# Two gates of an adaLN block: column sums on VectorE, spread over the partitions through DRAM

## The chip, the cores and the metric

The kernel runs on one core of a Trainium2 chip. The metric is the device time of one execution in microseconds (us). Engines are named as the profile names them: PE (TensorE), PEld (its weight loads), DVE (VectorE), ACT (ScalarE), POOL (GpSimd), SP (SyncE, which issues every DMA of this kernel). L12 is line 12 of the kernel before.

## What is computed

One block over x of shape (1, 2048, 512), with six rows of 512 made from a condition vector c of 512 elements:

```python
mod = (_silu(c) @ w_mod).reshape(c.shape[0], 6, 1, -1)
sa, ca, ga, sb, cb, gb = (mod[:, 0], mod[:, 1], mod[:, 2], mod[:, 3], mod[:, 4], mod[:, 5])
h = _layernorm(x, axis=-1) * (1 + ca) + sa
x = x + ga * _A_ref(h, A_w_r, A_w_i)      # rfft2, times w_r + i w_i, irfft2
h = _layernorm(x, axis=-1) * (1 + cb) + sb
x = x + gb * _B_ref(h, B_w1, B_b1, B_w2)  # 512 -> 1376, Mish, 1376 -> 512
return x
```

The two gates are ga and gb. Both multiply along the 512 features, which lie along the free axis of x in SBUF, so that each of the 128 partitions needs the whole row of 512.

## The kernel before

The work is three phases, each with a schedule written out by hand: an engine's instructions stand in the order of the program, and an instruction waits for semaphores of the others.

**First phase.** Forward transform over the features and over the long axis, one step for each of 16 slices of x. It also makes ca and sa.

**Second phase** (L534 to L596). The 64 complex columns are taken in 17 groups, in the order `seq`. In step s of its loop (L575) DVE multiplies group s with the spectral weights (`p2_prod`, L498), PE makes the products of group s+1 (`p2_mul`, L482), transposes group s+3 in (`p2_in`, L461), transposes group s-2 back (`p2_back`, L515) and makes the last products of group s-3 (`p2_out`, L528). POOL and, for a few groups, DVE combine the products to y (L503, L504). ACT copies the banks out (L464, L518) and stores d (L381, L382). A PSUM tag ("A" to "D") has two banks, so `p2_mul` of group s+1 waits until `p2_prod` of group s-1 has read its bank.

The rows 2 to 5 of `mod` are made beside it, in 16 pieces of w_mod of 128 x 512 (four for each row, 256 KB each). `mod_fetch(s + 2)` issues the loads into four buffers (L541), so a load waits for the sum four pieces earlier. `mod_late(s)` takes a piece on DVE, after `p2_prod` in program order; `when` (L534) gives the step of each piece: ga's four in steps 3, 4, 5 and 6, those of sb and cb in steps 6, 7, 8, 9, 9, 10, 11 and 12, and gb's four in steps 12, 13, 14 and 16. There are two forms:

- `mod_column` (L110), for sb and cb: a piece holds 128 of the features on its partitions and the 512 elements of the contraction along the free axis; one DVE instruction multiplies by silu(c), which lies on every partition (`scb`), and sums along the free axis into a column of `cols`.
- `mod_step` (L98 for the first piece, L100 for the others), for ga and gb: a piece holds 128 elements of the contraction on its partitions and the 512 features along the free axis; DVE multiplies it by silu(c) for each partition and adds it to a 128 x 512 accumulator, `modr[:, 0]` for ga and `modr[:, 2]` for gb.

The sum over the partitions that is left is a PE product with a 128 x 128 matrix of ones, which also puts the row on every partition: `mod_gate` (L553) in step 7 for ga, into a bank of tag "A", behind it `kiv`, the last transform's matrix, times the bank on DVE (L554); and `apply_gate` (L558) after the last step for gb, into a bank of tag "B", with a copy to `gbr` by ACT (L559). In step 9 SP issues the two loads of `kc` (1 MB each, L595), behind the eleventh piece of w_mod.

**Third phase** (L902 to L930). In 16 steps the inverse transform over the long axis with `kc` (`p3_col`, L663 and L664) and over the features with `kiv` (`p3_row`, L673), with x += (L676) and the second norm's sums. SP loads w1 in 12 pieces of up to 256 KB into two buffers (`load_w1`, L615; each is let go by `split_w1` of two pieces earlier, which ACT and POOL do in L621 and L622) and w2 (L703). Then follows the feed-forward part, in 8 blocks of 6 steps; `gbr` is first read there.

SP issues DMAs in program order; a DMA waits in the queue for what it needs, and those behind it wait too.

Of the kernel before, what the change touches and what calls it, by code (L numbers as in the profile page):

```python
# [31 lines left out]
def tile_spectral_block(ctx: ExitStack, tc: tile.TileContext, x_d, w1_d, b1_d, w2_d,  # L32
                        c_d, xt_d, wm_d, wq_d, wz_d, kr_d, km_d, kc_d, ki_d, kf_d, kv_d, kw_d, kp_d, out_d):
    nc = tc.nc
# [3 lines left out]
    base = ctx.enter_context(tc.tile_pool(name="base", bufs=1))  # L38
    small = ctx.enter_context(tc.tile_pool(name="small", bufs=4))
    work = ctx.enter_context(tc.tile_pool(name="work", bufs=2))  # L40
    big = ctx.enter_context(tc.tile_pool(name="big", bufs=1))

    psum = ctx.enter_context(tc.tile_pool(name="psum", bufs=2, space=bass.MemoryType.PSUM))

    def pipeline(count, *steps):
# [5 lines left out]
    def bank(tag):  # L51
        return psum.tile([P, 512], F32, name="bank", tag=tag)
# [8 lines left out]
    sc = base.tile([P, 4], F32, name="sc")  # L61
    ident = base.tile([P, P], F32, name="ident")
    kiv = base.tile([P, 4, P], F32, name="kiv")
    ones = base.tile([P, P], F32, name="ones")
    b1n = base.tile([P, NF], F32, name="b1n")
    modr = base.tile([P, 3, D], F32, name="modr")
    gbr = modr[:, 2]
    krs = modr[:, 0].rearrange("p (j e) -> p j e", j=4)
    scb = modr[:, 1]
    cols = base.tile([P, 2, 2, 4], F32, name="cols")  # L70
# [2 lines left out]
    nmr = base.tile([P, N2], F32, name="nmr")  # L73
    eps = base.tile([P, 1], F32, name="eps")

    saz = base.tile([P, NQ], F32, name="saz")
    mraw = big.tile([P, N2, 256], F32, name="mraw", tag="da")
    mring = big.tile([P, 8, 2, 384], F32R, name="mring", tag="db")
# [12 lines left out]
    kw = pw.tile([96, P], F32, name="kw")  # L91
    kb = modr[:, 2]
    hring = first.enter_context(tc.tile_pool(name="hring", bufs=1))

    def mod_step(acc, w, k, eng):
        one = sc[:, k:k + 1]
        if k == 0:
            eng.tensor_scalar(acc, w, one, 0.0, op0=ALU.mult, op1=ALU.add)  # L98
        else:
            eng.scalar_tensor_tensor(acc, w, one, acc, op0=ALU.mult, op1=ALU.add)  # L100

    def scale_spread():
        ps = bank("D")
# [5 lines left out]
    def mod_column(w, out, by, waste):  # L109
        nc.vector.scalar_tensor_tensor(waste, w, by, scb, op0=ALU.mult, op1=ALU.mult, accum_out=out)  # L110

    def plus_one(dst, src):
        nc.scalar.activation(dst, src, AF.Identity, bias=ones[:, 0:1])
# [45 lines left out]
    st = {}  # L159
# [294 lines left out]
    def p2_in(g):  # L454
        if g == 0:
            return z_in()
        q0, nq = groups[g]
        w = nq * P
        ps = bank("A")
        for i in range(nq):  # L460
            nc.tensor.transpose(ps[:, i * P:(i + 1) * P],  # L461
                                a_sb[:, q0 + i, :, :].rearrange("p n e -> p (n e)"), ident)
        z = zbuf(g)
        nc.scalar.copy(z[:, 0:w], ps[:, 0:w])  # L464
        st["z", g] = z
        if seq.index(g) >= 2:
            p2_shift(g)

    def p2_shift(g):
        q0, nq = groups[g]  # L470
        zc = st["z", g][:, 0:nq * P:P]
        nc.gpsimd.tensor_tensor(zc, zc, saz[:, q0:q0 + nq], op=ALU.add)

    def p2_mul(g):
        if g == 0:
            return z_mul()
        q0, nq = groups[g]
        w = nq * P
        z = st.pop(("z", g))
        pb = bank("B")  # L480
        for i in range(nq):
            nc.tensor.matmul(pb[:, 0:w].rearrange("p (e q) -> p e q", q=nq)[:, :, i], z[:, i * P:(i + 1) * P],  # L482
                             kf[:, 0:128], start=True, stop=True)
        st["pb", g] = pb
# [22 lines left out]
    def p2_back(g):  # L507
        if g == 0:
            return z_back()
        q0, nq = groups[g]  # L510
        w = nq * P
        y = st.pop(("y", g))
        pc = bank("C")
        for i in range(nq):
            nc.tensor.transpose(pc[:, i * P:(i + 1) * P], y[:, 0:w].rearrange("p (e q) -> p e q", q=nq)[:, :, i],  # L515
                                ident)
        t = buf("t")
        nc.scalar.copy(t[:, 0:w], pc[:, 0:w])  # L518
        st["t", g] = t
# [18 lines left out]
    def mod_fetch(s):  # L538
        for which, k in work_mod.get(s, ()):
            w = late[which, k] = hring.tile([P, 512], F32, name="wm", tag="ht", bufs=4)  # L540
            nc.sync.dma_start(w, wm_d[2 + which, k])  # L541

    def mod_late(s):
        for which, k in work_mod[s]:
            w = late.pop((which, k))
            if which in (1, 2):
                mod_column(w, cols[:, 1, which - 1, k:k + 1], 1.0, w)
            else:
                mod_step(modr[:, 0 if which == 0 else 2], w, k, nc.vector)

    def mod_gate():
        ga = bank("A")
        nc.tensor.matmul(ga, ones, modr[:, 0], start=True, stop=True)  # L553
        nc.vector.tensor_tensor(kiv, kiv, ga.rearrange("p (b a) -> p b a", b=4), op=ALU.mult)  # L554

    def apply_gate():
        gb = bank("B")
        nc.tensor.matmul(gb, ones, modr[:, 2], start=True, stop=True)  # L558
        nc.scalar.copy(gbr, gb)  # L559

    kc = []
    wqb = pw.tile([P, 8, 2, 64, 4], F32, name="wqb", tag="half")
    with tc.manual_schedule():
        for i in range(8):
            nc.sync.dma_start(wqb[:, i], wq_d[8 + i])
        for i in range(LEAD):
            p2_in(seq[i])
            if i == 1:
                for g in seq[:2]:
                    p2_shift(g)  # L570
            if i in (2, 4):
                p2_mul(seq[i // 2 - 1])
            if i == 3:
                p2_prod(seq[0])
        for s in range(len(seq) + 3):  # L575
            mod_fetch(s + 2)
            if 0 < s < len(seq):
                p2_prod(seq[s])
            if 2 <= s + 1 < len(seq):
                p2_mul(seq[s + 1])  # L580
            if LEAD <= s + 3 < len(seq):
                p2_in(seq[s + 3])
            mod_late(s)
            if 2 <= s < len(seq) + 2:
                p2_back(seq[s - 2])
            if s >= 3:
                p2_out(seq[s - 3])
            if s == 7:
                mod_gate()
            if s == 14:  # L590
                plus_one(cols[:, 1, 1, :], cols[:, 1, 1, :])
            if s == 9:
                for i, t in enumerate(("cr", "ci")):
                    kc.append(big.tile([P, N2, P], F32, name=f"kc{i}", tag=t))
                    nc.sync.dma_start(kc[i], kc_d[:, i, :, :])  # L595
        apply_gate()  # L596
    first.close()

    pm = ctx.enter_context(tc.tile_pool(name="pm", bufs=1))
# [8 lines left out]
    def piece(i):  # L608
        k, c = divmod(i, 3)
        return k, 512 * c, min(512 * c + 512, F)  # L610

    def load_w1(i):
        k, lo, hi = piece(i)
        r = buf("g2")[:, 0:hi - lo]
        nc.sync.dma_start(r, w1v[:, k, lo:hi])  # L615
        st["w1", i] = r
# [285 lines left out]
    for s in range(N2 + 1):  # L902
        if s < N2:
            p3_col(s)
        if s < 12:
            load_w1(s)
        if s >= 1:
            p3_row(s - 1)
        if s in (3, 5):
            norm_scale(s - 3, s - 1)  # L910
        if s in (9, 13):
            norm_scale(s - 5, s - 1)
        if s == 15:
# [140 lines left out]
def _layout(x, w_r, w_i, w_mod):  # L1054
    import numpy as np

    w = np.stack([w_r, w_i])
    p, k, q = np.arange(128), np.arange(16), np.arange(64)
    own = p[:, None] + 128 * k
    far = (128 - p[:, None] + 128 * k) % 2048  # L1060

    def pick(row, col):
        return w[:, row[:, :, None], col]

    wq = np.stack([pick(own, q), pick(own, q + 128), pick(far, 256 - q), pick(far, 128 - q)], 2)
    wz = np.concatenate([pick(own, np.array([0, 128])), pick(far, np.array([192, 64, 256]))], 3)
    wq = wq.reshape(2, 128, 4, 16, 16, 4).transpose(4, 1, 0, 2, 3, 5).reshape(16, 128, 2, 64, 4)
    m = w_mod.reshape(128, 4, 6, 512).transpose(2, 1, 0, 3).copy()
    m[1:3] = m[1:3].reshape(2, 4, 128, 128, 4).swapaxes(3, 4).reshape(2, 4, 128, 512)
    t = w_mod.reshape(128, 4, 6, 512).transpose(2, 3, 1, 0).reshape(6, 512, 512)  # L1070
    m[0] = t[0].reshape(128, 4, 512).swapaxes(0, 1)
    m[3:5] = t[3:5].reshape(2, 4, 128, 512)
    xt = x.reshape(128, 16, 128, 4).transpose(1, 2, 3, 0)
    out = dict(x_t=xt, w_mod=m, w_q=wq, w_z=wz.transpose(1, 0, 3, 2))
    return {k: np.ascontiguousarray(v) for k, v in out.items()}
# [28 lines left out]
```

## Time and profile before

| what | us |
|---|---|
| median of 3 runs | 391.72 |
| lowest and highest of them | 391.29, 391.91 |
| the profiled execution's own time | 391.52 |
| its span, first to last instruction | 389.4 |
| PE busy | 383.1 |
| DVE busy | 298.8 |
| ACT busy | 247.9 |
| POOL busy | 96.1 |

The span is what the profile's rows add up to; 2.1 us of the profiled execution's time lie outside it. A row of the timeline has the start, the duration, the engine, the line and operation, the result and its inputs, and in brackets how long the engine had been idle and what released it. A row of the groups by line has the number of instructions and their least, median and greatest duration in ns. The rows of DMA issues have the size of each and the median time from issue to landing. The chain that ended last is followed back from the last instruction to what released each one.

### The profile page before, as it was taken

The page shows a single profiled execution, that of the slowest core. Times are in us where ns is not written, and L with a number is a line of the kernel's source. Part 1 is how long each engine was busy: PE and PEld are TensorE (multiplying, and loading weights), DVE is VectorE, ACT ScalarE, POOL GpSimd, SP SyncE. Part 2 cuts the span into 40 slices and gives each one's busy share as a digit, 9 for nine tenths or more (in the row PEclk, how much of TensorE's full clock was granted, in tenths as well). Part 3 has the DMA queues.
Part 4 walks back from the last instruction along what each step waited for, and adds up shares of the span by engine and source line. Part 5 has one row for each costly group of instructions (what it writes and reads, how often), then busy time and mean ns, then how long its engine had stood idle before and what let it go on. Part 6 is the DMA issues. An engine that isn't in the chain of part 4 may idle for free.

```text
span 389.4 us, 7386 instructions
## 1 busy us (share of the span) xinstructions
PE 383.1 (98%) x2752; PEld 355.4 (91%) x2752; DVE 298.8 (77%) x668; ACT 247.9 (64%) x546; POOL 96.1 (25%) x132
## 2 busy tenths in 40 slices
PE   8999999999999999999999999999999999999996
PEld 8889889999999998999998998999999999899984
DVE  2888978876299989887856965965966875987993
ACT  1798756678559648975855765674674674594751
POOL 0687737665077533300000000000000010017000
PEclk9999999999999999999999999999999999999999
DMA  7999993472132411100100100100100200123011
GB/s 237 383 323 339 347 344 109 133 300 63 47 124 78 145 49 28 56 3 0 56 0 3 54 2 0 56 0 2 55 2 0 76 0 2 46 65 106 3 54 54
DMA packets 21027, 36.44 MB, mean 94 GB/s; under 512 B 3680, under 2 KB 6592, under 8 KB 20736
## 3 DMA queue, kind: packets, MB, share of 16 engines
q1 hardware_dynamic: 20992, 35.98, 27.1%
q8 instruction: 21, 0.34, 0.3%
q14 instruction: 14, 0.11, 0.1%
HBM read 31.78 MB, written 4.19 MB: 92 GB/s over the span
## 4 chain that ended last, share of the span: by engine, by line
PE 86%; DMA 4%; DVE 3%; ACT 3%; issue 1%; SPq 1%; POOL 1%; POOLq 0%; DVEq 0%
PE bank L805 24%; PE bank L752 20%; PE bank L754 10%; PE bank L482 3%; PE bank L528 3%; PE bank L673 3%; PE bank L663 3%; PE bank L664 3%; PE bank L797 2%; PE bank L248 2%; DMA x<-in_A_x_dram 2%; PE bank L203 2%; PE bank L817 2%; PE bank L642 2%; PE bank L461 2%; DMA mraw<-in_km_dram 2%
## 5 line engine op out<-in xcount | busy, mean ns | idle before, releaser
L762 ACT ACTIVATE buf<-bank,b1n 128x256 f32<-128x256 f32 (+1 forms) x88 | 40.8, 472 | 66.8 <-PE bank L754 66.4
L763 DVE TENSOR_TENSOR buf<-buf,bank 128x256 f32<-128x256 f32 (+1 forms) x88 | 35.4, 417 | 38.6 <-ACT buf L762 38.6
L715 DVE TENSOR_TENSOR al<-buf,ah 128x512 fp32r<-128x512 f32 (+2 forms) x85 | 53.5, 653 | 0.7 <-ACT ah L714 0.7
L734 POOL TENSOR_TENSOR buf<-buf,modr 128x512 f32<-128x512 f32 (+1 forms) x3 | 3.9, 1292 | 183.0 <-DMA buf<-in_B_w_dram 175.7
L752 PE MATMUL bank<-h2e,w1h 128*128 128x512 f32 (+1 forms) x176 | 48.4, 397 | 0.0
L752 PE MATMUL bank<-h2o,w1h 128*128 128x512 f32 (+1 forms) x176 | 48.3, 396 | 0.0
L714 ACT CAST ah<-buf 128x512 fp32r<-128x512 f32 (+2 forms) x85 | 43.0, 548 | 1.2 <-DVE buf L779 1.2
L779 DVE TENSOR_TENSOR buf<-buf 128x128 f32<-128x128 f32 x148 | 39.9, 311 | 3.5 <-ACT buf L769 2.2
L769 ACT ACTIVATE buf<-buf 128x512 f32<-128x512 f32 (+1 forms) x48 | 28.6, 596 | 14.8 <-DVE buf L763 14.7
L805 PE MATMUL bank<-w2a,ah 128*128 128x256 f32 x161 | 34.9, 286 | 0.0
L752 PEld LDWEIGHTS bank<-h2o,w1h 128*128 128x128 f32 (+1 forms) x176 | 30.2, 187 | 4.5
L752 PEld LDWEIGHTS bank<-h2e,w1h 128*128 128x128 f32 (+1 forms) x176 | 30.1, 187 | 4.5
L805 PE MATMUL bank<-w2b,ah 128*128 128x256 f32 x147 | 31.8, 283 | 0.0
L754 PEld LDWEIGHTS bank<-h2o,w1l 128*128 128x128 f32 (+1 forms) x176 | 26.7, 185 | 4.2
L754 PEld LDWEIGHTS bank<-h2e,w1l 128*128 128x128 f32 (+1 forms) x176 | 26.7, 185 | 4.2
L754 PE MATMUL bank<-h2e,w1l 128*128 128x256 f32 (+1 forms) x176 | 27.8, 280 | 0.0
L754 PE MATMUL bank<-h2o,w1l 128*128 128x256 f32 (+1 forms) x176 | 27.8, 280 | 0.0
L805 PEld LDWEIGHTS bank<-w2a,ah 128*128 128x128 f32 x161 | 26.7, 191 | 0.0
L663 PE MATMUL bank<-kc,d 128*128 128x128 f32 x128 | 24.7, 275 | 0.0
L664 PE MATMUL bank<-kc,d 128*128 128x128 f32 x128 | 24.7, 275 | 0.0
L805 PEld LDWEIGHTS bank<-w2b,ah 128*128 128x128 f32 x147 | 24.6, 191 | 0.0
L117 DVE BATCH_NORM_STATS2 st<-x 128x6 f32<-128x512 f32 x32 | 22.1, 689 | 0.8 <-DMA x<-in_A_x_dram 0.4
(227 smaller groups left out, 1002.7 us busy)
## 6 DMA issues: line engine op xcount, KB each, us to landing
buf<-in_B_w_dram SPq DMA_DIRECT2D x20, 256.0 KB, 2.8
x<-in_A_x_dram SPq DMA_DIRECT2D x16, 256.0 KB, 4.9
xring<-in_x_t_dram SPq DMA_DIRECT2D x16, 256.0 KB, 5.1
wm<-in_w_mod_dram SPq DMA_DIRECT2D x16, 256.0 KB, 4.2
out_dram<-x SPq DMA_DIRECT2D x7, 512.0 KB, 2.6
mraw<-in_km_dram SPq DMA_DIRECT2D x16, 128.0 KB, 5.0
wqa<-in_w_q_dram SPq DMA_DIRECT2D x8, 256.0 KB, 4.8
wqb<-in_w_q_dram SPq DMA_DIRECT2D x8, 256.0 KB, 5.5
```

Source lines behind the costliest of these rows:

```text
L117: nc.vector.bn_stats(t, x[:, n, :])
L663: nc.tensor.matmul(o, dj[:, 0:128], kc[0][:, n, :], start=True, stop=False)
L664: nc.tensor.matmul(o, dj[:, 64:192], kc[1][:, n, :], start=False, stop=True)
L714: nc.scalar.copy(h, r)
L715: nc.vector.tensor_tensor(l, r, plain(h), op=ALU.subtract)
L752: nc.tensor.matmul(ps, w1h[:, k, fs], h[:, k], start=(k == 0), stop=False)
L754: nc.tensor.matmul(ps[:, 0:256], w1l[:, k, fs], h[:, k, 0], start=False, stop=(k == 3))
L762: nc.scalar.activation(o, ps[:, 256:], AF.Identity, bias=b1n[:rows, f:f + 1])
L763: nc.vector.tensor_tensor(o, o, ps[:, 0:256], op=ALU.add)
L769: nc.scalar.activation(o, o, AF.Mish)
L779: nc.vector.tensor_tensor(o, p, q, op=op)
L805: nc.tensor.matmul(o, a[p][:, e], w2[t][q][:, r], start=(own and half == 0 and t == 1 and i == 0), stop=(end and i == 2 and (n, half) != ( ...
```

## The change

ga and gb are summed as columns, by `mod_column`, like sb and cb: their pieces of w_mod are laid out by feature, and the sums go to a new tile `gcol` of 128 x 2 x 4 (feature 4p + k on partition p). Then two DMAs turn the column into a row on every partition: `flat` writes the 128 x 4 elements, 16 bytes from each partition, to a DRAM tile of 512 elements; `spread` reads these 2 KB once for each of the 128 partitions into `modr[:, 0]` (ga) or `gbr` (gb). Both are issued by SP; the second waits for the first to land. For ga they are issued in steps 8 and 9 of the second phase (behind the tenth piece of w_mod, and behind the eleventh, in front of `kc`), and kiv's multiply moves from step 7 to step 12, behind that step's two pieces. It reads `modr[:, 0]` in SBUF in place of a bank. For gb they are issued in steps 2 and 4 of the third phase, each behind that step's load of w1. Both products with ones and ACT's copy go.

```diff
+    dram = ctx.enter_context(tc.tile_pool(name="dram", bufs=1, space=bass.MemoryType.DRAM))
+    def flat(name, src, k=4):
+        t = dram.tile([1, P * k], F32, name=name)
+        nc.sync.dma_start(t.rearrange("b (p k) -> p (b k)", k=k), src)
+        return t
+    def spread(dst, t):
+        nc.sync.dma_start(dst, bass.AP(tensor=t.tensor, offset=t.offset, ap=[[0, P], [1, D]]))
...
+    gcol = base.tile([P, 2, 4], F32, name="gcol")
...
     def mod_late(s):
         for which, k in work_mod[s]:
             w = late.pop((which, k))
-            if which in (1, 2):
-                mod_column(w, cols[:, 1, which - 1, k:k + 1], 1.0, w)
-            else:
-                mod_step(modr[:, 0 if which == 0 else 2], w, k, nc.vector)
+            mod_column(w, cols[:, 1, which - 1, k:k + 1] if which in (1, 2) else gcol[:, which // 3, k:k + 1], 1.0, w)
     def mod_gate():
-        ga = bank("A")
-        nc.tensor.matmul(ga, ones, modr[:, 0], start=True, stop=True)
-        nc.vector.tensor_tensor(kiv, kiv, ga.rearrange("p (b a) -> p b a", b=4), op=ALU.mult)
-    def apply_gate():
-        gb = bank("B")
-        nc.tensor.matmul(gb, ones, modr[:, 2], start=True, stop=True)
-        nc.scalar.copy(gbr, gb)
+        ga = modr[:, 0]
+        nc.vector.tensor_tensor(kiv, kiv, ga.rearrange("p (a b) -> p b a", b=4), op=ALU.mult)
...
-            if s == 7:
+            if s == 8:
+                st["ga"] = flat("ga", gcol[:, 0])
+            if s == 9:
+                spread(modr[:, 0], st["ga"])
+            if s == 12:
                 mod_gate()
...
-        apply_gate()
...
         if s < 12:
             load_w1(s)
+        if s == 2:
+            st["gb"] = flat("gb", gcol[:, 1])
+        if s == 4:
+            spread(gbr, st["gb"])
```

On the host, w_mod's rows for ga and gb are stored by feature, like those of sb and cb, instead of by element of the contraction.

More of the change, by code (lines that the diff above doesn't have):

```diff
@@ L93, in tile_spectral_block @@
     hring = first.enter_context(tc.tile_pool(name="hring", bufs=1))
[L95 to L98, printed above, removed]
-        else:
-            eng.scalar_tensor_tensor(acc, w, one, acc, op0=ALU.mult, op1=ALU.add)
     def scale_spread():
@@ L545, in mod_late @@
             w = late.pop((which, k))
-            if which in (1, 2):
-                mod_column(w, cols[:, 1, which - 1, k:k + 1], 1.0, w)
-            else:
-                mod_step(modr[:, 0 if which == 0 else 2], w, k, nc.vector)
+            mod_column(w, cols[:, 1, which - 1, k:k + 1] if which in (1, 2) else gcol[:, which // 3, k:k + 1], 1.0, w)
     def mod_gate():
-        ga = bank("A")
-        nc.tensor.matmul(ga, ones, modr[:, 0], start=True, stop=True)
-        nc.vector.tensor_tensor(kiv, kiv, ga.rearrange("p (b a) -> p b a", b=4), op=ALU.mult)
-    def apply_gate():
-        gb = bank("B")
-        nc.tensor.matmul(gb, ones, modr[:, 2], start=True, stop=True)
-        nc.scalar.copy(gbr, gb)
+        ga = modr[:, 0]
+        nc.vector.tensor_tensor(kiv, kiv, ga.rearrange("p (a b) -> p b a", b=4), op=ALU.mult)
     kc = []
@@ L1068, in _layout @@
     m = w_mod.reshape(128, 4, 6, 512).transpose(2, 1, 0, 3).copy()
-    m[1:3] = m[1:3].reshape(2, 4, 128, 128, 4).swapaxes(3, 4).reshape(2, 4, 128, 512)
+    m[1] = m[1].reshape(4, 128, 128, 4).swapaxes(2, 3).reshape(4, 128, 512)
     t = w_mod.reshape(128, 4, 6, 512).transpose(2, 3, 1, 0).reshape(6, 512, 512)
-    m[0] = t[0].reshape(128, 4, 512).swapaxes(0, 1)
+    for i in (0, 2, 5):
+        m[i] = t[i].reshape(128, 4, 512).swapaxes(0, 1)
     m[3:5] = t[3:5].reshape(2, 4, 128, 512)
```

## Prediction

> **What bounds the kernel now.** I read the chain that ended last, then the stage in which the gates are made. PE (TensorE) carries 86% of the chain; a product taken off PE is worth its length, as long as PE isn't then held by something else.
>
> ```profile
> PE 86%; DMA 4%; DVE 3%; ACT 3%; issue 1%; SPq 1%; POOL 1%; POOLq 0%; DVEq 0%
> ```
>
> Next the busy time by stretches, and the chain between 66 and 100 us. The columns of the first row are PE, PEld, DVE, ACT, POOL, granted clock, DMA share and GB/s. The gates' stage (second phase, 48 to 98 us) is in its middle a gapless row of PE work at the full clock (1.00), and both products with ones lie on the chain with 0.86 us each.
>
> ```profile
> 72.00:88.00 16.00, 16.00 (x144) 16.00 (x144) 13.52 (x28) 11.76 (x36) 11.51 (x19) 1.00 0.68 247
> ```
>
> ```profile
> 71.13 0.86 PE bank L553 x2
> ...
> 98.22 0.86 PE bank L558 x2
> ```
>
> The chain names what was last, not what was nearly last. For that I read the timeline around each place. Numbers in brackets there are idle time before the instruction and its releaser.
>
> **The first product (L553), removed.** The timeline at step 7 of the second phase:
>
> ```profile
> 69.72 1.29 DVE L498 TENSOR_TENSOR buf<-bank,wqa 128x512 f32<-128x512 f32 x2
> ...
> 70.97 1.02 PE L553 MATMUL bank<-modr,ones 128*128 128x512 f32 x2
> ...
> 71.83 1.05 PE L482 MATMUL bank<-kf,buf 128*128 128x128 f32 x8
> 72.03 0.69 DVE L554 TENSOR_TENSOR kiv<-kiv,bank 128x512 f32<-128x512 f32 x1 [0.42 <-PE bank L553]
> ```
>
> Without L553, the L482 products behind it (p2_mul of step 9's group) could start at 70.97, if their bank were free. That is a "B" bank, and there are two: it is let go by the L498 pair that ends at 69.72 + 1.29 = 71.01. So they start at about 71.04 in place of 71.83: **0.79 us gained**. DVE also loses its wait on PE (0.42) and the multiply L554 at this place, so it is about a microsecond earlier too and holds nobody up here. With PE in a gapless row until 88, the 0.79 stays until something holds PE.
>
> **The second product (L558) and the copy L559, removed.** At the seam to the third phase:
>
> ```profile
> 98.25 0.37 ACT L381 COPY d<-bank 128x256 f32<-128x256 f32 x1 [0.34 <-PE bank L528]
> ...
> 98.68 0.43 PEld L663 LDWEIGHTS bank<-kc,d 128*128 128x128 f32 x2 [0.43 <-ACT d L381]
> 98.92 0.38 PE L663 MATMUL bank<-kc,d 128*128 128x128 f32 x2
> 99.11 0.62 ACT L559 COPY modr<-bank 128x512 f32<-128x512 f32 x1
> ...
> 100.95 0.59 ACT L666 COPY buf<-bank 128x512 f32<-128x512 f32 x1 [1.22 <-PE bank L664]
> ```
>
> Here the chain's 0.86 is misleading. L663's weights wait for ACT's copy of d (98.62), which has nothing to do with the gate, and load at 98.68. Without L558 the first product follows its weights at once, some 0.1 later, instead of at 98.92: **0.15 us gained**, between 0.1 and 0.24. The copy L559 lies in time in which ACT then waits 1.22 for PE: nothing. Both products together: 0.94.
>
> **The columns on DVE.** Eight sums change form: L98 and L100 go, eight more of L110, each with a read of its accumulator.
>
> ```profile
> L98 DVE TENSOR_SCALAR modr<-wm,sc x2: 479/584/690, 59.8 to 85.1; 128x512 f32<-128x512 f32 x2
> L100 DVE SCALAR_TENSOR_TENSOR modr<-wm,sc,modr x6: 739/805/1223, 60.6 to 93.9; 128x512 f32<-128x512 f32 x6
> L110 DVE SCALAR_TENSOR_TENSOR wm<-wm,modr x8: 680/694/1211, 66.1 to 83.6; 128x512 f32<-128x512 f32 x8
> L110 DVE DVE_READ_ACCUMULATOR wm<-wm,modr x8: 75/78/84, 67.2 to 84.2; 128x1 f32 x8
> ```
>
> By medians that is 2 x 0.58 + 6 x 0.81 = 6.0 before and 8 x (0.69 + 0.08) = 6.2 after, beside PE work: nothing by itself.
>
> **The moved multiply, and the place where it lands.** kiv's multiply goes from step 7 to step 12, behind the twelfth and thirteenth pieces of w_mod. In those two pieces DVE waits for transfers today:
>
> ```profile
> 83.61 0.69 DVE L110 SCALAR_TENSOR_TENSOR wm<-wm,modr 128x512 f32<-128x512 f32 x1 [1.08 <-DMA wm<-in_w_mod_dram]
> ...
> 85.06 0.69 DVE L98 TENSOR_SCALAR modr<-wm,sc 128x512 f32<-128x512 f32 x1 [0.76 <-DMA wm<-in_w_mod_dram]
> 85.67 1.28 DVE L498 TENSOR_TENSOR buf<-bank,wqb 128x512 f32<-128x512 f32 x2
> ...
> 88.04 1.06 PE L482 MATMUL bank<-kf,buf 128*128 128x128 f32 x8
> ```
>
> The L498 pair of step 13 ends at 86.95 and frees the bank for the products at 88.04: today it has 1.09 to spare. After the change PE would be there at 88.04 - 0.79 = 87.25. DVE, if the thirteenth piece lands as now, starts its sum at 85.06, the multiply at 85.67, the pair at 85.67 + 0.61 = 86.28 (0.61 is the step from L98's start to the next), ends at 87.56, and PE goes at 87.60. **PE is held 0.35**: the cover of 1.09 was used up by PE's own gain and by the multiply. Queued behind the multiply on DVE are the products of steps 13 to 16, and PE waits for them through the banks.
>
> To it comes what POOL and DVE do to each other. The multiply now reads two SBUF tensors, where L554 read a bank, and the thirteenth sum becomes an L110, which also reads two:
>
> ```profile
> 65.59 1.18 POOL L504 TENSOR_TENSOR buf<-buf 128x256 f32<-128x256 f32 x1
> ...
> 66.10 1.21 DVE L110 SCALAR_TENSOR_TENSOR wm<-wm,modr 128x512 f32<-128x512 f32 x1
> ...
> 85.43 0.91 POOL L504 TENSOR_TENSOR buf<-buf 128x256 f32<-128x256 f32 x1
> ```
>
> Beside a POOL instruction an L110 took 1.21 instead of 0.69. Step 12's L504 moves with PE to about 84.65 to 85.5 and overlaps the sum at 85.06 by some 0.4: a cost of 0 to 0.5, and I take 0.2, since the overlap is partial. [...]
>
> **The round trip through DRAM, first gate.** SP issues in order, so its rows, and those of DMA issues with their time to landing, say who is pushed back:
>
> ```profile
> 41.49 0.43 SPq L189 DMA_DIRECT2D kiv<-in_ki_dram  x1
> 42.30 0.38 SPq L190 DMA_DIRECT2D b1n<-in_B_b_dram  x1
> ...
> 71.64 0.33 SPq L541 DMA_DIRECT2D wm<-in_w_mod_dram  x1
> ...
> 74.55 0.33 SPq L541 DMA_DIRECT2D wm<-in_w_mod_dram  x1
> 74.98 0.38 SPq L595 DMA_DIRECT2D kc<-in_kc_dram  x1
> ...
> 76.99 0.33 SPq L541 DMA_DIRECT2D wm<-in_w_mod_dram  x1
> ```
>
> ```profile
> wm<-in_w_mod_dram SPq DMA_DIRECT2D x1, 256.0 KB, 2.6
> wm<-in_w_mod_dram SPq DMA_DIRECT2D x1, 256.0 KB, 8.0
> sc<-in_c_dram SPq DMA_DIRECT2D x1, 2.0 KB, 1.6
> kiv<-in_ki_dram SPq DMA_DIRECT2D x1, 256.0 KB, 5.1
> b1n<-in_B_b_dram SPq DMA_DIRECT2D x1, 5.0 KB, 4.6
> ```
>
> The 71.64 row is the tenth piece (landing after 2.6, at 74.3), 74.55 the eleventh, 76.99 the thirteenth (landing after 8.0, at 85.0: it stands behind the 2 MB of kc). The 2 KB write of the column is issued behind the tenth piece, at 72.0. No write of this kind is in the trace. Its bounds are 1.6 (sc, the same shape, on an empty queue) and 4.6 (b1n, small packets on a loaded one). b1n was issued 0.8 after kiv (42.30, 41.49) and landed only 0.3 after it (46.9, 46.6): a small transfer lands just behind the large one ahead of it. So I take 74.3 + 0.35 = 74.65. SP then waits, in front of the spread read and so of kc: the read is issued at 74.65, kc at about 75.05 instead of 74.98. The eleventh piece is issued a microsecond earlier than now, since the sum that frees its buffer is; so the 256 KB of the spread read take the place in the queue that this piece has today. The thirteenth piece lands 0.05 later. With the bounds: 73.6 to 76.6 for the write, that is kc 0.9 earlier to 2.0 later; a spread read that is slow, because it reads the same 2 KB 128 times, comes on top of it and has no row; by the rows of full loads (2.6 on a free queue) it is none.
>
> The sum: 0.94 gained, less a hold of 0.35 + 0.2 + 0.05 = 0.60, leaves about 0.35.
>
> **The round trip, second gate.** It is issued in the third phase, between loads that wait for buffers anyway:
>
> ```profile
> 107.91 5.89 SPq L615 DMA_DIRECT2D buf<-in_B_w_dram  x3
> 113.90 0.85 SPq L703 DMA_DIRECT2D buf<-in_B_w_dram  x2
> 117.36 3.69 SPq L615 DMA_DIRECT2D buf<-in_B_w_dram  x2
> ...
> 119.72 0.49 ACT L621 CAST w1h<-buf 128x352 fp32r<-128x352 f32 x1
> 120.51 1.02 ACT L650 ACTIVATE buf<-bank,cols 128x256 f32<-128x256 f32 x2 [0.30 <-PE bank L642]
> ```
>
> The write goes after the first of the three at 107.91, in SP's wait for the next buffer. The read goes before the pair at 113.90, and SP has time until 117.36. It could delay the 117.36 load, used at 119.72, by a few tenths; ACT's 0.30 of waiting at 120.51 covers that. Nothing, at most 0.4.
>
> **The rivals.** *Full gain:* the write lands by 74.2, or kc's bytes flow faster with pieces issued closer together; the thirteenth piece lands 0.5 earlier, and PE isn't held. 391.72 - 0.94 = 390.8. For it: the hold is short. Against it: the write stands behind the tenth piece. *Gain eaten:* the L110 beside L504 costs the whole 0.5 and the multiply meets POOL too, the hold is about 0.85, and 391.6 is left. *Slower, by a late round trip:* SP stands in front of kc until the column is in DRAM, each microsecond of that moves the thirteenth piece, and through DVE's order the products at 88.04, by as much. At 0.35 later than I take it nothing is gained; from 1.15 later (392.5) the kernel is slower by more than 0.2%; with b1n's 4.6, 1.95 later, it is +1.6: 393.3. Against it: b1n had a queue full of large loads before it, the column has one piece. [...] That the change does not take place can be excluded: both products are gone from PE's list of instructions.
>
> **How the numbers follow.** The profiled execution took 391.52 with a span of 389.4, 0.2 under the median of 391.72; the 0.35 come off the median: **391.3**. Chances: forecast 0.48, full gain 0.22, gain eaten 0.14, late round trip past its point of 1.15 later 0.16. About 0.2% (0.8 us) is what a measurement can tell from no change: faster 0.22, same 0.48 + 0.14 = 0.62, slower 0.16. The range, 390.7 to 392.7, takes in the full gain and reaches just past the point of the late round trip, whose rest it leaves out.
>
> **What would show it.** L482 follows L403 with no gap but 0.1 (first product). DVE waits for w_mod around 83.6 and 85, then multiply and pair, and PE idles about 0.6 before the L482 of step 14, with L498 as releaser: that is the hold. No hold means the full gain. A kc issue later than 75.5 means the late round trip. L663 within 0.15 of its weights shows the second product. Wrong would be a PE gap in steps 8 to 12, or one around 120 us put down to w1.

## The result, and the profile after

The changed kernel takes **396.19 us** (median of 6 runs, 394.88 to 398.66); beside it the kernel before takes 391.58 (6 runs, 390.90 to 391.91). The ratio is 1.0122 [1.0101, 1.0142]: slower by 1.2%, where 391.3 was forecast. The profiled execution took 394.88 with a span of 393.1, which is 3.36 more than the profiled execution before (391.52).

The page of the changed kernel, its span and the shares of the chain by engine, answers to the first line of the prediction. The share of DMA in the chain went from 4% to 7%.

```profile
span 393.1 us, 7393 instructions
...
PE 83%; DMA 7%; DVE 4%; ACT 2%; issue 1%; SPq 1%; POOL 1%; POOLq 0%; DVEq 0%
```

The same stretch as before (72 to 88 us) by engine, then the two stretches that turn out to matter (columns: PE, PEld, DVE, ACT, POOL, granted clock, DMA share, GB/s). PE is no longer busy throughout; it does nothing from 86.8 to 89.7, and in the 3.4 us after that it is busy at a granted clock of 0.50.

```profile
72.00:88.00 16.00, 14.79 (x132) 14.59 (x130) 10.41 (x23) 12.37 (x36) 9.87 (x17) 1.00 0.76 247
```

```profile
86.80:89.70 2.90, 0.00 (x0) 0.01 (x1) 2.90 (x6) 1.00 (x4) 0.00 (x0) 1.00 0.30 99
89.70:93.10 3.40, 3.38 (x16) 3.40 (x17) 3.40 (x8) 0.39 (x1) 2.66 (x4) 0.50 0.00 0
```

Next the timeline of the changed kernel at the places of the prediction's steps. Its lines stand four behind those of before in this part: L403 became L407, L482 became L486, L498 L502, L110 L114; further down, L663 became L661.

```profile
69.94 0.39 PE L407 MATMUL bank<-kv,buf 128*128 128x128 f32 x2
70.33 1.13 PE L486 MATMUL bank<-kf,buf 128*128 128x128 f32 x8
...
83.92 1.06 PE L486 MATMUL bank<-kf,buf 128*128 128x128 f32 x8
...
86.08 0.69 DVE L114 SCALAR_TENSOR_TENSOR wm<-wm,modr 128x512 f32<-128x512 f32 x1 [4.97 <-DMA wm<-in_w_mod_dram]
...
86.70 0.69 DVE L114 SCALAR_TENSOR_TENSOR wm<-wm,modr 128x512 f32<-128x512 f32 x1
...
87.32 1.06 DVE L554 TENSOR_TENSOR kiv<-kiv,modr 128x512 f32<-128x512 f32 x1
...
88.30 1.27 DVE L502 TENSOR_TENSOR buf<-bank,wqb 128x512 f32<-128x512 f32 x2
...
89.72 2.05 PE L486 MATMUL bank<-kf,buf 128*128 128x128 f32 x8 [2.94 <-DVE buf L502]
...
101.61 0.37 ACT L385 COPY d<-bank 128x256 f32<-128x256 f32 x1 [0.34 <-PE bank L532]
102.03 0.30 PEld L661 LDWEIGHTS bank<-kc,d 128*128 128x128 f32 x2 [0.65 <-ACT d L385]
102.03 0.49 PE L661 MATMUL bank<-kc,d 128*128 128x128 f32 x2 [0.46 <-DMA buf<-in_B_w_dram]
```

One row of before that the prediction does not show is needed to place them, the last products in front of the removed one:

```profile
70.75 0.39 PE L403 MATMUL bank<-kv,buf 128*128 128x128 f32 x2
```

Set the same instructions side by side (after less before). The products in front of the removed one: 69.94 - 70.75 = -0.81; this execution is already ahead by its first phase, where nothing was changed (over the fourteen profiled executions these products start between 69.94, here, and 71.93). Those behind it: 70.33 - 71.83 = -1.50, so **0.69 gained**. Step 14's products: 89.72 - 88.04 = +1.68, so **3.18 lost in one place**, 2.94 of it as idle time of PE, with DVE's pair L502 as releaser. The first product of the third phase: 102.03 - 98.92 = +3.11. The removed second product gave 0.25 there (the product follows the copy of d by 0.05 instead of 0.30), so between the two places 3.11 - 1.68 + 0.25 = **1.68 was lost without any wait**: that is the stretch at half clock, in which eight L486 take 2.05 instead of 1.06, and half of 3.4 us is 1.7. At 382 us the distance is still +3.19. The spans differ by 3.7, so about 0.5 more comes at the very end.

Why does DVE come late at 88.30? It stands idle for 4.97 us in front of 86.08, for the twelfth piece of w_mod. SP's rows and the landings show where that piece was:

```profile
70.82 0.33 SPq L545 DMA_DIRECT2D wm<-in_w_mod_dram  x1
71.20 0.42 SPq L47 DMA_DIRECT2D ga<-gcol  x1
72.65 0.33 SPq L545 DMA_DIRECT2D wm<-in_w_mod_dram  x1
73.67 0.33 SPq L51 DMA_DIRECT2D modr<-ga  x1
74.10 0.85 SPq L594 DMA_DIRECT2D kc<-in_kc_dram  x2
75.04 1.11 SPq L545 DMA_DIRECT2D wm<-in_w_mod_dram  x1
```

```profile
kc<-in_kc_dram SPq DMA_DIRECT2D x2, 1024.0 KB, 9.6
...
modr<-ga SPq DMA_DIRECT2D x1, 256.0 KB, 5.6
ga<-gcol SPq DMA_DIRECT2D x1, 2.0 KB, 2.5
```

The write of the column is issued at 71.20 and lands 2.5 later; the spread read is issued at 73.67, the moment the write has landed, and kc at 74.10. Before, kc was issued at 74.98. Of this 0.88, 0.81 is the lead that the execution brings from its first phase: beside PE's row, kc is issued where it was before, and still it lands later. These are the landings of its two halves, before and after (least, median and greatest time from issue):

```profile
DMA to landing us min/median/max: 5.0/6.0/7.1
```

```profile
DMA to landing us min/median/max: 8.4/9.6/10.8
```

The rates say how. The view of the DMA engines between 70 and 90 us has 40 slices of half a microsecond: the first row is the engines' busy share in tenths, the second what they moved. Before:

```profile
DMA  0000058200099989999999989999617480000000
GB/s 0 0 0 0 0 123 307 94 0 0 0 135 360 438 311 393 442 426 426 442 393 459 422 332 381 393 373 406 229 61 111 139 307 8 0 0 0 0 0 0
```

After:

```profile
DMA  0007691020859999898999989979999921017700
GB/s 0 0 0 45 106 353 24 0 98 0 49 180 328 98 127 106 188 447 360 475 410 410 459 344 442 442 299 426 393 397 397 344 86 53 29 25 217 283 0 0
```

Before, the row is near 400 GB/s from the thirteenth slice (76.0) on. After, it reaches that in the eighteenth (78.5), 2.5 us later; in the four slices from 76.5 the engines are 80% busy and more, and move 98 to 188 GB/s. The pieces behind kc are late with it. The twelfth, before and after:

```profile
wm<-in_w_mod_dram SPq DMA_DIRECT2D x1, 256.0 KB, 7.2
```

```profile
wm<-in_w_mod_dram SPq DMA_DIRECT2D x1, 256.0 KB, 11.0
```

The thirteenth piece lands 10.4 after its issue at 76.24, at 86.68; before, it landed 8.0 after 76.99, at 85.04.

### The profile page after: what moved, and what is told of

Read it like the earlier page. It is cut to its first block, busy times and chain, and to the rows that moved or that the text cites. A ratio compares the mean times of both kernels' runs of the same rounds, so it can differ in the third digit from the quotient of the medians.

```text
span 393.1 us, 7393 instructions
## 1 busy us (share of the span) xinstructions
PE 383.1 (97%) x2748; PEld 356.5 (91%) x2748; DVE 299.2 (76%) x676; ACT 247.3 (63%) x545; POOL 96.1 (24%) x132
## 4 chain that ended last, share of the span: by engine, by line
PE 83%; DMA 7%; DVE 4%; ACT 2%; issue 1%; SPq 1%; POOL 1%; POOLq 0%; DVEq 0%
PE bank L803 24%; PE bank L750 20%; PE bank L752 10%; DMA wm<-in_w_mod_dram 3%; PE bank L671 3%; PE bank L486 3%; PE bank L661 3%; PE bank L662 3%; PE bank L795 2%; PE bank L252 2%; PE bank L207 2%; DMA x<-in_A_x_dram 2%; PE bank L815 2%; PE bank L532 2%; PE bank L640 2%; DMA mraw<-in_km_dram 1%
## 5 line engine op out<-in xcount | busy, mean ns | idle before, releaser
L661 PE MATMUL bank<-kc,d 128*128 128x128 f32 x128 | 24.8, 276 | 0.5 <-DMA buf<-in_B_w_dram 0.5
```

The lines of the kernel that those rows point to most:

```text
L661: nc.tensor.matmul(o, dj[:, 0:128], kc[0][:, n, :], start=True, stop=False)
```

## The experiments

Twelve kernels ran in three groups, each group beside the kernel before on the same chip (medians 391.41, 391.73 and 391.51 us). The theory that I formed from the profile after was that the spread read is slow *because it reads one row of 2 KB 128 times* and keeps kc back; its main rival was that *any* load of 256 KB at that place does so. A second question was whether the clock at one half is part of the loss.

**One gate at a time.** *ga_only* is the changed kernel with the second gate as before (sum in rows, product with ones, copy); *gb_only* has only the second gate changed. The sums and the product with ones of the gate that is left as before are not shown here.

```diff
 ga_only
-        if s == 2:
-            st["gb"] = flat("gb", gcol[:, 1])
-        if s == 4:
-            spread(gbr, st["gb"])
...
+        apply_gate()
 gb_only
-            if s == 8:
-                st["ga"] = flat("ga", gcol[:, 0])
-            if s == 9:
-                spread(modr[:, 0], st["ga"])
-            if s == 12:
+            if s == 7:
                 mod_gate()
...
```

> The other half: the first gate through DRAM with kiv's multiply in step 12, the second by its product with ones as before. All theories: nearly the whole loss of the full change, +4.5 us against the kernel before (ratio 1.0115), with DVE waiting some 5 us for the twelfth piece, a PE gap of about 3 us in front of step 14's products, and a clock of 0.5 for some 3 us behind it. Theory (same row) sees the read of the row land 5 us or more after its issue again.

> Half of the change: the second gate through DRAM, the first by its product with ones as before. All theories put the loss at the first gate's place: L558 goes, 0.15 to 0.25 gained at the seam, at most 0.3 lost to the second read in the third phase. Ratio 0.9995 (391.4), PE gapless in the second phase, clock 1.0. If it is slower by 0.5 us or more, the second gate's round trip has a price of its own.

Measured: ga_only 396.15, ratio 1.0104 [1.0068, 1.0140]; gb_only 391.53, ratio 0.9993 [0.9979, 1.0007]. The whole loss is the first gate's; the second round trip, whose write landed 2.1 and whose read 4.2 us after its issue in the changed kernel, costs nothing. The timeline of ga_only shows the hold again, with 2.44 us of idle time (L493 there is L486). The half clock that was expected behind it is not in this execution, whose mean clock is 1.000:

```profile
90.20 1.02 PE L493 MATMUL bank<-kf,buf 128*128 128x128 f32 x7 [2.44 <-DVE buf L509]
```

**Does the read hold kc back, and is it the one row?** Three kernels. *b1_same_row* and *b2_own_rows* are the kernel before, with products, sums and multiply as they were, and one read of 256 KB more, in front of kc, that nobody uses: 128 times the same 2 KB of c, or 128 rows of their own. *own_rows* is the changed kernel in which the spread is replaced by a read of 128 rows of w_mod, which does not wait for the write; the first gate's row is not made then.

```diff
 b1_same_row
+                nc.sync.dma_start(modr[:, 0], bass.AP(tensor=c_d.tensor, offset=c_d.offset, ap=[[0, P], [1, D]]))
                 for i, t in enumerate(("cr", "ci")):
 b2_own_rows
+                nc.sync.dma_start(modr[:, 0], wm_d[2, 0])
                 for i, t in enumerate(("cr", "ci")):
 own_rows
-                spread(modr[:, 0], st["ga"])
+                nc.sync.dma_start(modr[:, 0], wm_d[2, 0])
```

> The kernel before, with one read more in front of the two kc loads: 128 reads of one 2 KB row (the input c), into a part of modr that is free by then; nothing uses it. Theory (same row): the read itself is slow because every partition's 2 KB come from one address. It lands 4 to 6 us after issue instead of 2.6, the thirteenth piece of w_mod lands at about 87 instead of 85.0, DVE's order passes that on, and PE is held about 1 us in step 14: ratio about 1.0025, without a drop of the clock (the idle stretch is too short) or 1.006 with one. Rival (fresh write): reading what was written just before through 16 B packets is slow; here nothing was written, so the read lands in about 2.7 and the time is unchanged. Rival (bytes and order): any 256 KB in front of kc cost 0.7, less than the 1.09 that step 13 has to spare: unchanged.

> The kernel before, with one read more in front of the two kc loads: 128 different rows of 2 KB (a piece of w_mod), into the same free part of modr; nothing uses it. Theory (same row): lands 2.6 to 3 us after issue, the thirteenth piece at about 85.7, no hold of PE: ratio 1.000. Rival (bytes and order): the same as the read of one row, whatever that gives.

> The full change, with the spread read of the column (one 2 KB row read 128 times) replaced by a read of 128 own rows of w_mod at the same place in the queue; the small write stays, but nothing waits for it. The first gate's values are not the reference's then. Theory (same row): the read lands after 3 us instead of 5.6, kc and the pieces 1 to 2 us sooner than in the full change, ratio 1.006 instead of 1.012. Rival (any read there): as the full change, 1.012.

Measured: b1_same_row 393.57, ratio 1.0068 [1.0042, 1.0095]; b2_own_rows 394.25, ratio 1.0063 [1.0046, 1.0080]; own_rows 394.24, ratio 1.0064 [1.0036, 1.0091]. In front of step 14's products PE idles 1.14, 2.22 and 1.84 in their profiles, at the whole clock. **My theory fell with b2_own_rows**: rows of their own cost the kernel before as much as the same row 128 times (its profiled execution, 395.73, is the slowest of its ten). The DMA issues of b1_same_row, then of b2_own_rows, have the read in question, and kc:

```profile
modr<-in_c_dram SPq DMA_DIRECT2D x1, 256.0 KB, 4.8
```

```profile
kc<-in_kc_dram SPq DMA_DIRECT2D x2, 1024.0 KB, 9.7
...
modr<-in_w_mod_dram SPq DMA_DIRECT2D x1, 256.0 KB, 3.1
```

The read of own rows lands after 3.1, that of the one row after 4.8; yet kc takes 9.7 behind the first (median of the two), and b1_same_row's kc 8.9. Before it took 6.0. The rates of the two kernels, from 70 to 90 us in half microseconds, first b1_same_row, then b2_own_rows:

```profile
DMA  0000027800045996452679999999899999630485
GB/s 16 0 0 0 0 66 139 307 12 0 0 66 213 389 246 37 41 61 78 279 311 442 442 393 459 426 410 426 344 385 369 406 406 361 234 143 25 78 238 209
```

```profile
DMA  4300000577000389955989969899999998643210
GB/s 176 143 0 0 0 0 0 82 160 279 4 0 0 106 291 270 430 197 229 279 295 311 279 197 360 328 426 393 373 377 381 389 406 324 234 193 127 98 45 25
```

They lose the time in different ways. With the same row, four slices from 77.5 move 37 to 78 GB/s, and two slices later the rate is above 400. With own rows the rate never falls so low, but stays between 197 and 311 for 3.5 us from 78.5, with the engines between half and fully busy. By bytes alone 256 KB more would cost 256 KB / 410 GB/s = 0.64 us, an estimate with the 410 GB/s of several slices above. own_rows gives back about half of the changed kernel's loss (1.0064 beside 1.0122), some of it because its hold of 1.84 didn't lower the clock in its profiled execution; the other half is there without any row being read twice. The one row does have a price of its own: the read lands 2.36 behind the eleventh piece in the changed kernel (79.30 and 76.94) and 0.67 in own_rows (78.83 and 78.16), near the 0.64 of its bytes. It is a part, not the whole cause.

**Is it the place in front of kc?** *behind* has b2's read behind the two loads of kc, ahead of the twelfth piece. *tiny_front* has a read of 2 KB, 16 bytes for each partition, in front of kc. *write_front* has only the write of 2 KB, at step 8, and no read. All three are the kernel before with that one addition.

```diff
 behind
                     nc.sync.dma_start(kc[i], kc_d[:, i, :, :])
+                nc.sync.dma_start(modr[:, 0], wm_d[2, 0])
 tiny_front
+                nc.sync.dma_start(modr[:, 0, 0:4], c_d.rearrange("b (p k) -> p (b k)", k=4))
                 for i, t in enumerate(("cr", "ci")):
 write_front
+            if s == 8:
+                flat("ga", sc)
```

> The kernel before, with the read of 128 own rows of 2 KB (256 KB, used by nothing) behind the two kc loads and in front of the twelfth piece, instead of in front of kc. Theory (it is the place in front of kc that costs, not the bytes): kc lands after 5 and 7 us, the two pieces 0.7 later, at 84.3 and 85.7, less than the 1.09 to spare: ratio 1.000, PE without a hold. Rival (bytes in the queue cost wherever they stand, some 2.5 us for 256 KB): as with the read in front, ratio 1.006.

> The kernel before, with a read of 2 KB (128 packets of 16 bytes) in front of the two kc loads, into a free part of modr; nothing uses it. Theory (bytes in front of kc): 2 KB do nothing, kc lands after 5 and 7 us, ratio 1.000. Rival (any DMA more in front of kc, by its count or its small packets): kc lands 2 to 4 us later than before, ratio about 1.006 as with the two 256 KB reads.

> The kernel before, with the 2 KB write alone (128 x 16 bytes from SBUF to a DRAM tile, silu(c) as data, read by nobody) at step 8's place behind the tenth piece of w_mod. Theory (small write): the eleventh piece lands 4 us after its issue instead of 2.7, kc 7 and 10 us after theirs, the thirteenth piece at about 87, PE held about 1 us: ratio 1.0025. Rival (issue time of the eleventh piece): that piece is issued at 74.5 as before, everything lands as before, ratio 1.000.

Measured: behind 392.21, ratio 1.0015 [0.9994, 1.0036]; tiny_front 392.34, 1.0018 [0.9999, 1.0037]; write_front 392.11, 1.0009 [0.9991, 1.0026]. None of them shows PE idle in front of step 14's products, but all hold it a little: these products start 2.89 to 2.90 behind step 13's, before it was 2.70 (88.04 and 85.34). The times of kc from issue to landing in behind, tiny_front and write_front, in this order:

```profile
DMA to landing us min/median/max: 4.9/5.9/6.9
```

```profile
DMA to landing us min/median/max: 5.8/6.8/7.8
```

```profile
DMA to landing us min/median/max: 5.4/6.8/8.1
```

The same 256 KB behind kc leave kc as it was (5.9 beside 6.0) and cost about a tenth of a per cent or nothing; in front of it they cost 0.6%. The thirteenth piece stands behind the read in both kernels. In behind it lands at 85.63, 0.6 later than before (85.04), which is what the bytes take by the same estimate; in b2_own_rows it lands at 89.75, 3.5 later even without the 1.18 by which that execution's first phase is late. With a write or read of 2 KB in front, kc takes 0.8 longer, which the slack in front of step 14 covers but for 0.2. Little of this 0.8 is certain: in gb_only, with nothing more in front of kc than before, it took

```profile
DMA to landing us min/median/max: 5.0/6.5/8.0
```

For write_front neither what the theory nor what the rival expected came out: the eleventh piece, right behind the write, landed 3.4 after its issue (2.7 before, 4 expected), and PE was held 0.2, not 1.

**Moving the round trip away from kc.** *late_spread* is the changed kernel with the read in step 14 and the multiply in step 17; the write stays in front of kc. *late_both* has the write in step 14, the read in 16 and the multiply in 18. *mul17* leaves both transfers in front of kc and only moves the multiply from step 12 to 17.

```diff
 late_spread
-            if s == 9:
+            if s == 14:
                 spread(modr[:, 0], st["ga"])
-            if s == 12:
+            if s == 17:
                 mod_gate()
 late_both
-            if s == 8:
+            if s == 14:
                 st["ga"] = flat("ga", gcol[:, 0])
-            if s == 9:
+            if s == 16:
                 spread(modr[:, 0], st["ga"])
-            if s == 12:
+            if s == 18:
                 mod_gate()
 mul17
-            if s == 12:
+            if s == 17:
                 mod_gate()
```

> The full change, but the read that spreads the first gate is issued in step 14, behind the last piece of w_mod, and kiv's multiply is in step 17, where DVE is idle. The 2 KB write stays in front of the eleventh piece. Theory (one more read in front of kc keeps kc and the pieces behind it back, whichever rows it reads): kc lands 5 and 7 us after issue again, DVE waits only as in the kernel before, no hold of PE beyond 0.1, clock 1.0: the 0.9 of the two products is gained, ratio 0.9977, 390.7. Rival (the round trip itself, its small write or the column sums, costs): slower than the kernel before by some us as in the full change.

> The full change with the first gate's whole round trip behind the last piece of w_mod: the 2 KB write in step 14, the spread read in step 16, kiv's multiply in step 18, where DVE is idle. Theory (small write in front of kc keeps back the eleventh piece and kc, as in the run with the late read): without it kc lands 5 and 7 us after issue as before, the twelfth piece before 83.6, PE's hold in front of step 14's products goes from 0.47 to 0, and the two products' 0.9 are gained: ratio 0.9977, 390.8. Rival (it is not the write: kc is slow whenever the eleventh piece is issued a microsecond sooner, as it is in every kernel without the first product with ones): kc lands 7 and 10 us after issue again, hold of about 0.5, ratio 1.000.

> The full change with kiv's multiply in step 17 instead of 12, the read still in front of kc. The pieces land as late as in the full change (theory: kc kept back), but DVE goes on to step 13's products about 1 us sooner, so PE's gap is 1.9 instead of 2.9 us. If the clock halves only after a gap longer than that, about 2.6 us of the 4.6 are given back (393.6, ratio 1.005); if the clock halves all the same, 1.0 us (395.2, ratio 1.009). Rival (the multiply's place is what costs): back to 391.5.

Measured: late_spread 392.24, ratio 1.0005 [0.9988, 1.0023]; late_both **391.06, ratio 0.9983 [0.9966, 1.0000]**; mul17 393.53, ratio 1.0044 [1.0025, 1.0063]. The landing of kc in late_spread, then in late_both:

```profile
DMA to landing us min/median/max: 6.9/8.4/9.9
```

```profile
DMA to landing us min/median/max: 4.9/6.2/7.5
```

With both transfers out of the way kc lands as before (6.2 beside 6.0), and the kernel is the fastest of all, about half of the forecast 0.94 below the kernel before, at the edge of what the interval can tell. Its trace has the gain: from the last products in front of the removed one to the first of the third phase it takes 27.34 (70.39 to 97.73), before it took 28.17 (70.75 to 98.92). The rates say the same: late_both moves about 400 GB/s from 75.0 on.

```profile
DMA  0000286098989999999989999710892000967830
GB/s 0 0 0 0 45 225 250 4 164 299 422 344 426 426 410 393 426 410 393 414 352 381 406 442 373 270 57 25 143 357 61 0 0 0 41 45 180 156 102 0
```

late_spread fell short of what I expected: with the write alone in front, kc still takes 8.4, though write_front's took only 6.8 with such a write. The write slows the load behind it: the eleventh piece takes 3.4 to 4.4 from issue to landing in the seven profiled kernels with the write in front of it (4.2 here), and 2.65 to 2.71 in the seven without. late_spread's remaining hold, and that of mul17, are in their timelines (late_spread first):

```profile
84.62 1.27 DVE L114 SCALAR_TENSOR_TENSOR wm<-wm,modr 128x512 f32<-128x512 f32 x1 [2.91 <-DMA wm<-in_w_mod_dram]
...
87.86 1.13 PE L486 MATMUL bank<-kf,buf 128*128 128x128 f32 x8 [0.47 <-DVE buf L502]
```

```profile
90.13 1.13 PE L486 MATMUL bank<-kf,buf 128*128 128x128 f32 x8 [1.93 <-DVE buf L502]
```

In mul17 the multiply is gone from in front of step 14's pair and PE waits 1.93 instead of 2.94, one multiply (0.98) less; the eight products behind the wait take 1.13, so the clock is whole. The kernel gave back 2.66: about a microsecond is the multiply, and the rest, 1.7, is as much as the half clock took.

**Is the clock a part of it?** *warm14* is the changed kernel with 14 pairs of products of ones, whose result nobody uses, in PE's gap ahead of step 14's products.

```diff
+            if s == 14:
+                warm(14, "A")
             if 2 <= s + 1 < len(seq):
                 p2_mul(seq[s + 1])
```

> The full change with 14 products of ones with ones (128 x 128, into a free bank that nothing reads) on PE in front of step 14's products, about 3 us of work in PE's gap. The hold itself stays (DVE sets it). Theory (the gap makes the clock halve): clock 1.0 throughout, 1.6 us given back: 394.6, ratio 1.008. Rival (the lower clock comes for another reason): clock 0.99 as in the full change, 396.2 or more.

Measured: 394.14, ratio 1.0059 [1.0031, 1.0087]. Its timeline:

```profile
88.00 3.29 PE L293 MATMUL bank<-ones 128*128 128x128 f32 x28
91.12 1.06 PE L486 MATMUL bank<-kf,buf 128*128 128x128 f32 x8
```

The gap is filled, the eight products behind it take 1.06, and the kernel is 2.05 faster than the changed one, though it does more work and waits as long. The two profiled executions (395.21 here, 394.88 for the changed kernel) don't show that in their times, since this one's first phase ended 1.37 later, and what follows the second phase took 0.6 longer. Between the same two rows as above they do:

```profile
71.31 0.39 PE L407 MATMUL bank<-kv,buf 128*128 128x128 f32 x2
...
101.78 0.49 PE L663 MATMUL bank<-kc,d 128*128 128x128 f32 x2 [0.46 <-ACT d L385]
```

That is 30.47; the changed kernel took 32.09 (69.94 to 102.03), 1.62 more, and the half clock was put at 1.68. What is left of the median's loss, about 2.4 over the kernel before, is the hold less the gains: 3.18 - 0.69 - 0.25 = 2.24.

## Why the prediction was wrong, point by point

- **First product removed: right.** 0.79 forecast, 0.69 measured; L486 follows L407 without a gap (69.94 + 0.39 = 70.33).
- **Second product and copy: right.** 0.15 forecast (0.1 to 0.24), 0.25 measured, just above the bound; weights and product of L661 start together. That both products together come to the 0.94 of the forecast is luck: 0.10 less for the first, 0.10 more for the second.
- **Columns on DVE: right.** The sixteen sums took 0.70 in the median (0.68 to 1.22), and no other engine waited for one before step 14.
- **Second gate: right.** Nothing forecast, 0.9993 [0.9979, 1.0007] for gb_only.
- **The place of the hold: right.** In front of step 14's products, with DVE's pair as releaser and the multiply and the pieces of w_mod in front of the pair. Its size: 0.60 forecast, 3.18 measured.
- **The step that failed** is the round trip's price in the queue: "so the 256 KB of the spread read take the place in the queue that this piece has today" (the eleventh), "The thirteenth piece lands 0.05 later", together with "by the rows of full loads (2.6 on a free queue) it is none". I counted the queue in bytes and in SP's issue times. The issue times held: kc was issued at 74.10, which is 74.91 without the lead of 0.81, where I forecast 75.05. But on the way kc's halves took 3.4 and 3.7 us longer than before, the twelfth piece 3.8 and the thirteenth 2.4. The thirteenth piece landed at 86.68 instead of 85.04; with the lead counted in, that is 2.45 later and not 0.05. Its sum was to start 2.19 ahead of the time at which PE is ready for step 14 (85.06 and 87.25); it started 0.16 behind it (86.70, and 88.04 - 1.50 = 86.54). That is 2.35 of the missing 2.58. The price from the row of a load on a free queue could not show this, and I took "none" as a value without keeping a bound above it in the range. behind, b2_own_rows and late_both show that it is the place in front of kc that costs. That kc is then slower by more than the bytes is shown; why is not (below).
- **The moved multiply: mis-sized.** 0.61 forecast, 0.98 measured (87.32 to 88.30): 0.37 more. I took the step of L98, with one tensor as input; the multiply has two, one of them read in steps of four elements. The sums also have two inputs in SBUF and took 0.69, so two inputs alone don't make the difference; the steps are my guess, and no run tests them. POOL was idle then, so it wasn't the term that I had kept for POOL; that term (0.2) was not needed, the two sums took 0.69.
- **The hold adds up**: 0.35 forecast without POOL and round trip, 2.35 for the late piece, 0.37 for the multiply, 0.11 from the pair's end to the products (89.57 to 89.72, instead of 0.04): 3.18.
- **What was not in the sum at all**: the half clock behind the gap, 1.68. I priced a hold at its length. warm14 and mul17 show the price: with the gap filled the eight products behind it take 1.06, and behind a gap of 1.93 they take 1.13, where the changed kernel's took 2.05 behind 2.94. Behind ga_only's gap of 2.44 the clock stayed whole as well (1.000 in the mean of that execution). Whether the gap's length alone decides, and from where between 2.44 and 2.94, no run shows.
- **The rival "slower, by a late round trip"** had the direction and not the mechanism: SP didn't stand in front of kc for longer than today, and the write landed 2.5 after its issue, 0.16 behind the tenth piece (73.49), where I had 0.35. That the write slows the eleventh piece behind it (4.3 instead of 2.7) is the smaller part, as late_spread's 1.0005 shows.
- **The range** ended at 392.7, just past this rival's point, and had no case in which kc is issued in time and lands late.

Two things stay open. First, what in the queue makes kc slow behind another transfer: the rates show engines that idle, or that are busy and move a fraction of the usual bytes, but not which engine worked on which transfer, and by the estimate from the bytes only 0.64 us are explained. late_spread and write_front, both with the write alone in front of kc, differ by 1.6 in kc's landing; no run separates what else differs there (the eleventh piece is issued 0.8 before the write has landed in late_spread, 0.3 after it in write_front, for one). Second, the median of the changed kernel is 4.61 over before, the profiled execution 3.36. Of the 1.25 between them, 0.81 is the lead of the profiled execution's first phase, which is no part of the change. The other executions show mean clocks of 0.991 to 0.996, and a stretch of 3.4 us at one half takes 0.0043 off the mean, so by this estimate one or two such stretches; but one execution at a clock of 1.000 took 396.31, with a span of 393.7 beside the profiled 393.1, so the clock isn't all of their difference.

## What to carry to other kernels

A small transfer put ahead of a large one in a queue is to be priced by when the large one lands, not by its own bytes: look for the consumer behind the large load, and put the small ones behind it if their result isn't due yet (here, with the multiply out of the way in both, the same two DMAs came out at 1.0044 [1.0025, 1.0063] ahead of kc, in mul17, and at 0.9983 [0.9966, 1.0000] behind it, in late_both). A hold of an engine that is always busy can cost more than its length (here PE's idle 2.94 us were followed by a granted clock of 0.50, which cost 1.68 more), so bound it with the clock behind it. Where the trace has no row for how transfers disturb each other, the upper bound belongs in the range.

## What the runs showed of the hardware that was not expected

- PE's granted clock fell to 0.50 for 3.4 us behind an idle stretch of 2.94 us. Behind stretches of 2.44 (ga_only), 2.22 (b2_own_rows), 1.93 (mul17) and less it did not in the profiled executions.
- A load of 256 KB in front of 2 MB, on one queue, moved the landing of the 2 MB from 6.0 to 9.7 us after issue (b2_own_rows); behind it, to 5.9 (behind).
- Reading one 2 KB row for 128 partitions took 4.8 to 5.6 us to land, 128 rows of their own 3.1 to 4.7 at the same place. Behind the last piece of w_mod the one row took 3.1 (late_spread) and 3.8 (late_both).
- A 2 KB write, 16 bytes from each partition, from SBUF to DRAM landed 2.5 us after its issue behind one load of 256 KB (changed kernel), and the load of 256 KB right behind such a write took 3.4 to 4.4 to land, without it 2.65 to 2.71.
- DVE's multiply of two SBUF tensors, 128x512 with one read in steps of four elements, took 1.06 with POOL idle (1.06 to 1.12 in the seven kernels that have it); with the second operand in a bank it had taken 0.69.
